# A causal linear attention with two expert layers behind it: earlier routing of the first token group, state products by halves

## The chip, the cores and the metric

The kernel runs on one core of one Trainium2 chip. The metric is the device time of one launch in microseconds (us); less is better. A time is the median of several runs, and a profile is one execution of its own.

## What is computed

The input of the expert layers is a gated linear attention: 4 batches of 8 heads, 768 positions, head size 48. Its output, 3072 rows of 384, goes through a layer of 8 experts of which each row takes the best two, and then through a gated product layer.

```python
for t in range(S):
    state = alpha[:, :, t, :, None] * state + np.einsum('bhd,bhe->bhde', k[:, :, t], v[:, :, t])
    y[:, :, t] = np.einsum('bhd,bhde->bhe', q[:, :, t], state)
...
logits = x @ w_gate
noise_scale = np.log1p(np.exp(x @ w_noise))
noisy_logits = logits + noise_scale * noise
top2 = np.argpartition(-noisy_logits, 2, axis=1)[:, :2]
...
    h = np.maximum(x[mask] @ w1[e], 0.0)
    out[mask] += top2_w[mask, k, None] * (h @ w2[e])
...
return (a * b @ w_out).astype(np.float32)      # a = x @ w_a, b = x @ w_b
```

## The kernel before

The order of all work is written out by hand: each engine runs its instructions in the order in which the program emits them, and waits only where data needs it.

**Attention.** The rows are cut into 24 tiles of 128 positions, six per batch. The loop over the tiles i emits for each: the load of tile i+5; `t_unit(i+1)`, four TensorE transposes of the keys (L664), with a filling product of no use (`fill`, L628) in front from tile `FILL` on; `gx_unit(i-1)`, three transposes of the output of the last tile (L749), likewise with a filling product; `inter(i)`, the queries times the state of the past (L688, the state lies as a block-diagonal copy `Sbd`, and it is left out for the first tile of a batch); `sc_unit(i+1)`, the scores (L672), masked by VectorE (L677); `prep(i+3)`, two scans on VectorE (L640, L644) and the products with them on GpSimd (L642, L645, L648); `intra(i)`, the masked scores times the values (L696); the copy of the output on ScalarE (L704); `gm_unit(i-1)`, the logits (L758), and their copy (`lg_unit`, L763, ScalarE); `sbd(i+1)`, two copies of the state into `Sbd` (L714, ScalarE); `u_unit(i+1)`, keys times values (L725); `s_unit(i+1)`, which adds them to the state on VectorE (L740, or L737 in a batch's first tile) and scales it on GpSimd (L741); and `w_tick(i)`, the split of an expert weight on ScalarE and GpSimd (L114, L115). A weight is split into a rounded part and a rest, as the expert products take three passes (L829 to L831).

**Routing beside it.** `routing(s)` is a Python generator. It joins a list when the logits of a subset of tiles are through: subset 0 is tiles 0 to 13, subset 1 tiles 14 to 18, subset 2 tiles 19 to 23. Each call of `tick` resumes every generator on the list up to its next `yield`, and so fixes where its instructions stand in the engines' queues. The loop calls `tick` four times a tile, numbered 0 to 3: ahead of `inter`, behind `prep`, ahead of `u_unit`, and behind `s_unit`. Write (i, k) for tick k of tile i. `choose` makes the noisy logits and the two best experts (ScalarE, then GpSimd, then VectorE; on VectorE alone for the last subset). `route` of a group (group 0 is subset 0, group 1 the other two) ranks its rows by a scan (L337) and products (L345 to L351), makes places from them (VectorE L356 to L384, TensorE L393), and gathers the rows of expert 0 with indirect DMAs that GpSimd issues (L493). `lists` makes the row lists of the other experts: equality tables on VectorE (L440, L444) and products (L460), whose sum goes into one accumulator (L463). `before_states` holds products back until tick 2 or the end of the loop. After the loop, `tick` is called from the expert units.

**Behind the loop.** `x_unit(0, j)` transposes a block of gathered rows (L501); blocks 0 and 1 stand inside tile 23, between `inter(23)` and `intra(23)`. Then come three filling products, the logits of tile 23, and expert 0 with its first 384 rows, `up_unit(0, f, 0)`, in which L829 starts.

```python
    def before_states():
        while phase[0] in (0, 1, 3):
            yield
...
    def tick(k=None):
        phase[0] = k
        for d in side[:]:
            if next(d, 0) == 0:
                side.remove(d)
```

Of the kernel before, what the change touches and what calls it, by code (L numbers as in the profile page):

```python
# [21 lines left out]
NT = B * NCH  # L22
# [20 lines left out]
LAG = 3  # L43
# [5 lines left out]
FILL = 13  # L49
# [12 lines left out]
def moe_kernel(ctx: ExitStack, tc, qka, afirst, v, wgn, noise, w1, w2, w3, out):  # L62
# [183 lines left out]
    def choose(s):  # L246
# [29 lines left out]
        for _ in hop(1):  # L276
            yield
        nc.scalar.activation(c, w, AF.Copy, bias=-1.0)
        nc.scalar.activation(mz, z, AF.Relu)
        for _ in hop(2, 1):  # L280
            yield
# [6 lines left out]
        for _ in hop(4):  # L288
            yield
# [3 lines left out]
        for k in range(2):  # L293
            eq = scr("eq", E)
            m, mk = (tl(rt, [128, MCH], F32, f"r_{x}{k}", bufs=2)[:, :n] for x in ("m", "mk"))
            o = oh[k][:, i0:i1]
            nc.vector.tensor_reduce(m, nl, axis=AX.X, op=ALU.max)
            for _ in hop(1):
                yield
            nc.vector.tensor_tensor(eq, nl, m[:, :, None].to_broadcast(sh), op=ALU.is_equal)  # L300
            nc.vector.tensor_tensor(eq, eq, prio[:, None, :].to_broadcast(sh), op=ALU.mult)
            for _ in hop(1):
                yield
            nc.vector.tensor_reduce(mk, eq, axis=AX.X, op=ALU.max)
            nc.vector.tensor_tensor(o, eq, mk[:, :, None].to_broadcast(sh), op=ALU.is_equal)
            yield
            if k == 0:
                nl2 = scr("nl2", E)
                nc.vector.scalar_tensor_tensor(nl2, o, -1e30, nl, op0=ALU.mult, op1=ALU.add)
                nl = nl2  # L310
            ms.append(m)
# [3 lines left out]
        for _ in hop(2, 1):  # L315
            yield

    def route(g):
# [21 lines left out]
        for _ in range(LAG + 1 if last else LAG):  # L340
            yield
# [46 lines left out]
        for _ in range(LAG - 1 if last else LAG):  # L388
            yield
# [31 lines left out]
    def lists(g):  # L421
# [27 lines left out]
        for s, after in zip(sets, sets[1:] + [None]):  # L449
# [6 lines left out]
            yield from before_states()  # L456
# [107 lines left out]
    def routing(s):  # L564
        yield from choose(s)
        g = group_of[CHS[s]][0]
        if CHS[s + 1] == groups[g][-1] + 1:
            yield from route(g)
            yield from lists(g)
# [14 lines left out]
    with ExitStack() as actx:  # L584
# [98 lines left out]
        def inter(i):  # L683

            PY[i] = bank(4)
            if i % NCH:
                for p in range(NP):
                    nc.tensor.matmul(PY[i][:, p * 96:p * 96 + 96], ring[i % RING][:, p * 128:p * 128 + 128],  # L688
                                     Sbd[i % 2][:, p], start=p == 0, stop=False, skip_group_check=True)
# [92 lines left out]
        for i in range(NT):  # L782
# [18 lines left out]
            x_out_unit(i)  # L801
            if i > 0:
                lg_unit(i - 1, gm_unit(i - 1))
            sbd(i + 1)
# [532 lines left out]
```

## Time and profile before

| | us |
|---|---|
| median of 3 runs (lowest, highest) | 1017.1 (1016.07, 1017.14) |
| the profiled execution | 1016.42 |
| its span, first to last instruction | 1014.6 |
| TensorE busy | 987.8 (97%) |
| VectorE busy | 557.0 (55%) |
| GpSimd busy | 416.4 (41%) |
| ScalarE busy | 376.1 (37%) |

The profile is of one execution. PE is TensorE's products, PEld its weight loads, DVE VectorE, ACT ScalarE, POOL GpSimd; L12 is line 12 of the program. A product of 32-bit floats has two records. Products overlap, so the time of one is better read from the start of one group to the start of the next. Attention ends, and expert 0 starts, at 138 us of the span.

### The profile page before, as it was taken

To read this page: it belongs to the slowest core of one execution; us is meant where nothing else is said; L and a number is where in the kernel's file an instruction comes from. 1 tells how busy PE (TensorE), PEld (TensorE's weight loads), DVE (VectorE), ACT (ScalarE), POOL (GpSimd) and SP (SyncE) were. 2 spreads that over 40 slices of the span, in tenths; PEclk is the share of its full clock that TensorE was granted. 3 is DMA by queue.
4 is the path that set the end of the run, shared out by engine and by line. 5 is a ranking of instruction groups with operands and counts; after the bars stand their busy time and mean duration, and the time that the engine had idled before them with its cause. 6 is when DMAs were issued, how large, how long until landed. Compare 5 with 4: busy or idle time off the path is not lost.

```text
span 1014.6 us, 17331 instructions
## 1 busy us (share of the span) xinstructions
PE 987.8 (97%) x6544; PEld 895.6 (88%) x6544; DVE 557.0 (55%) x967; ACT 376.1 (37%) x811; POOL 416.4 (41%) x433
## 2 busy tenths in 40 slices
PE   6999979999999999999999999999999999999997
PEld 5998868999999999999999888888888888888886
DVE  8998855576766776766756454333332333433221
ACT  2455521554545454545444343222222222222222
POOL 7688712575867685868564334020020110000000
PEclk9999989999999999999999999999999999999999
DMA  9787111668687868787856444140140240120100
GB/s 337 265 310 278 54 40 36 199 195 243 218 229 225 227 209 241 232 233 237 221 151 195 120 141 109 45 111 0 47 109 1 56 102 1 32 62 1 32 1 34
DMA packets 126549, 141.44 MB, mean 139 GB/s; under 512 B 76512, under 2 KB 110432, under 8 KB 126432
## 3 DMA queue, kind: packets, MB, share of 16 engines
q1 hardware_dynamic: 119904, 120.13, 39.6%
q0 software_dynamic: 6528, 19.67, 6.5%
q8 instruction: 83, 1.36, 0.6%
q14 instruction: 34, 0.28, 0.1%
HBM read 101.43 MB, written 38.34 MB: 138 GB/s over the span
## 4 chain that ended last, share of the span: by engine, by line
PE 83%; DVE 2%; DMA 1%; ACT 1%; issue 1%; POOL 0%; SPq 0%; DVEq 0%; ACTq 0%; POOLq 0%
PE bank L829 27%; PE bank L831 27%; PE bank L830 26%; DMA row<-xd,idx 1%; PE bank L501 1%; DMA wd<-w 1%; PE bank L696 1%; PE bank L460 0%; DVE HB L881 0%; PE bank L672 0%; PE bank L688 0%; PE bank L628 0%; DVE u L980 0%; ACT HB L880 0%; ACT o L1171 0%
## 5 line engine op out<-in xcount | busy, mean ns | idle before, releaser
L829 PE MATMUL bank<-HB,W 128*128 128x416 f32 (+5 forms) x564 | 201.3, 357 | 2.2 <-ACT HB L880 1.5
L831 PE MATMUL bank<-HB,W 128*128 128x416 f32 (+5 forms) x564 | 200.0, 355 | 0.0
L830 PE MATMUL bank<-HB,W 128*128 128x416 f32 (+5 forms) x564 | 199.8, 354 | 0.0
L115 POOL TENSOR_TENSOR W<-wst,W 128x384 fp32r<-128x384 f32 x136 | 146.8, 1088 | 91.9 <-ACT W L114 80.2
L1148 DVE TENSOR_TENSOR p<-bank,a 128x512 f32<-128x512 f32 x72 | 49.8, 692 | 236.1 <-PE bank L831 236.1
L829 PE MATMUL bank<-X,W 128*128 128x416 f32 (+6 forms) x474 | 166.3, 351 | 0.6 <-ACT X L503 0.4
L831 PE MATMUL bank<-X,W 128*128 128x416 f32 (+5 forms) x474 | 165.3, 349 | 0.0
L830 PE MATMUL bank<-X,W 128*128 128x416 f32 (+5 forms) x474 | 165.3, 349 | 0.0
L1010 POOL DMA_INDIRECT row<-y,row x48 | 46.3, 964 | 200.4 <-DVE row L1018 167.0
L829 PEld LDWEIGHTS bank<-HB,W 128*128 128x128 f32 x564 | 106.1, 188 | 9.8 <-ACT HB L880 2.6
L831 PEld LDWEIGHTS bank<-HB,W 128*128 128x128 f32 x564 | 105.9, 188 | 7.4 <-POOL W L115 0.2
L830 PEld LDWEIGHTS bank<-HB,W 128*128 128x128 f32 x564 | 106.0, 188 | 7.2
L1146 ACT ACTIVATE a<-bank 128x512 f32<-128x512 f32 x72 | 43.1, 598 | 168.5 <-PE bank L831 168.5
L1150 ACT ACTIVATE HB<-p 128x512 fp32r<-128x512 f32 x72 | 45.5, 632 | 157.6 <-DVE p L1148 157.6
L880 ACT ACTIVATE HB<-bank 128x416 fp32r<-128x416 f32 (+2 forms) x128 | 65.8, 517 | 100.7 <-PE bank L831 100.5
L829 PEld LDWEIGHTS bank<-X,W 128*128 128x128 f32 x474 | 89.1, 188 | 5.1 <-DVE HB L881 0.7
L881 DVE SCALAR_TENSOR_TENSOR HB<-bank,HB 128x416 fp32r<-128x416 f32 (+2 forms) x128 | 72.6, 582 | 36.9 <-ACT HB L880 36.3
L831 PEld LDWEIGHTS bank<-X,W 128*128 128x128 f32 x474 | 89.0, 188 | 3.9
L830 PEld LDWEIGHTS bank<-X,W 128*128 128x128 f32 x474 | 89.0, 188 | 3.8
L114 ACT ACTIVATE W<-wst 128x384 fp32r<-128x384 f32 x144 | 72.3, 516 | 17.4 <-DMA wst<-w 15.8
L493 POOL DMA_INDIRECT row<-xd,idx x56 | 57.8, 1033 | 47.9 <-DVE r_t L407 24.5
L1151 DVE TENSOR_TENSOR HB<-p,HB 128x512 fp32r<-128x512 f32 x72 | 49.8, 692 | 50.3 <-ACT HB L1150 50.3
(236 smaller groups left out, 1727.1 us busy)
## 6 DMA issues: line engine op xcount, KB each, us to landing
wst<-w SPq DMA_DIRECT2D x128, 192.0 KB, 4.5
ring<-qka SPq DMA_DIRECT2D x22, 768.0 KB, 6.3
wd<-w SPq DMA_DIRECT2D x36, 384.0 KB, 4.7
y<-o SPq DMA_DIRECT2D x56, 156.0 KB, 3.2
xt<-tb SPq DMA_DIRECT2D x11, 768.0 KB, 4.8
raw<-xt SPq DMA_DIRECT2D x44, 192.0 KB, 4.4
w3f<-u SPq DMA_DIRECT2D x36, 192.0 KB, 3.0
wst<-w3f SPq DMA_DIRECT2D x36, 192.0 KB, 3.2
```

The source lines that it names most:

```text
L114: nc.scalar.activation(h, raw, AF.Copy)
L115: eng.tensor_tensor(l, raw, h.bitcast(F32), op=ALU.subtract)
L493: nc.gpsimd.indirect_dma_start(out=t[:m], out_offset=None, in_=xd[:SPLIT * 128] if a else xd, in_offset=bass.IndirectOffsetOnAxis(ap=ix, a ...
L829: nc.tensor.matmul(ps[:, :m], ah, bh[:, :m], start=first, stop=False)
L830: nc.tensor.matmul(ps[:, :n], ah, bl[:, :n], start=False, stop=False)
L831: nc.tensor.matmul(ps[:, :n], al, bh[:, :n], start=False, stop=last)
L880: nc.scalar.activation(Hh[:, f, s], pu[:, :n], AF.Relu)
L881: nc.vector.scalar_tensor_tensor(Hl[:, f, s], pu[:, :n], 0.0, Hh[:, f, s].bitcast(F32), op0=ALU.max, op1=ALU.subtract)
L1010: nc.gpsimd.indirect_dma_start(out=t, out_offset=None, in_=src, in_offset=bass.IndirectOffsetOnAxis(ap=row[:, i, k:k + 1], axis=0))
L1148: nc.vector.tensor_tensor(p, ps[1], a, op=ALU.mult)
L1150: nc.scalar.activation(h, p, AF.Copy)
L1151: nc.vector.tensor_tensor(l, p, h.bitcast(F32), op=ALU.subtract)
```

## The change

`choose` yields less often for the subsets that aren't the last; `route` waits one tick less in two places of group 0; `lists` of group 0 waits for the end of the loop, and each set of a list but the last gives way for two ticks ahead of its product, in place of `before_states`. The filling products start at tile 17 instead of 13. `inter` does each product as two of 64 queries. The copy of the logits is emitted behind the copies into `Sbd`.

```diff
-FILL = 13
+FILL = 17
@@ choose
         nc.scalar.activation(r, ln, AF.Exp, scale=-1.0)
-        for _ in hop(1):
-            yield
         nc.scalar.activation(c, w, AF.Copy, bias=-1.0)
         nc.scalar.activation(mz, z, AF.Relu)
-        for _ in hop(2, 1):
+        for _ in hop(1, 1):
             yield
...
-        for _ in hop(4):
+        for _ in hop(3):
             yield
...
             nc.vector.tensor_reduce(m, nl, axis=AX.X, op=ALU.max)
-            for _ in hop(1):
-                yield
             nc.vector.tensor_tensor(eq, nl, m[:, :, None].to_broadcast(sh), op=ALU.is_equal)
             nc.vector.tensor_tensor(eq, eq, prio[:, None, :].to_broadcast(sh), op=ALU.mult)
-            for _ in hop(1):
-                yield
             nc.vector.tensor_reduce(mk, eq, axis=AX.X, op=ALU.max)
             nc.vector.tensor_tensor(o, eq, mk[:, :, None].to_broadcast(sh), op=ALU.is_equal)
-            yield
+            if k == 0 or last:
+                yield
...
-        for _ in hop(2, 1):
+        for _ in hop(1, 1):
             yield
@@ route
-        for _ in range(LAG + 1 if last else LAG):
+        for _ in range(LAG + 1 if last else LAG - 1):
             yield
...
-        for _ in range(LAG - 1 if last else LAG):
+        for _ in range(LAG - 1):
             yield
@@ lists
             m, at, bt = hot.pop(s)
-            yield from before_states()
+            if s[1] != NT:
+                yield
+                yield
@@ routing
             yield from route(g)
+            while phase[0] is not None:
+                yield
             yield from lists(g)
@@ inter
-                    nc.tensor.matmul(PY[i][:, p * 96:p * 96 + 96], ring[i % RING][:, p * 128:p * 128 + 128],
-                                     Sbd[i % 2][:, p], start=p == 0, stop=False, skip_group_check=True)
+                    for t in (0, 64):
+                        nc.tensor.matmul(PY[i][t:t + 64, p * 96:p * 96 + 96],
+                                         ring[i % RING][:, p * 128 + t:p * 128 + t + 64],
+                                         Sbd[i % 2][:, p], start=p == 0, stop=False, skip_group_check=True)
@@ the loop over the tiles
-            if i > 0:
-                lg_unit(i - 1, gm_unit(i - 1))
-            sbd(i + 1)
+            pg = gm_unit(i - 1) if i > 0 else None
+            sbd(i + 1)
+            if i > 0:
+                lg_unit(i - 1, pg)
```

## Rows read from the trace of the kernel before

**Rows 1.** TensorE's waits: who it waited for; us in total, times, longest.

```profile
PE bank L501 <- DMA row<-xd,idx: 3.1, 2, 2.4
PE bank L688 <- ACT Sbd L714: 2.0, 3, 1.0
...
PE bank L460 <- DVE lacc L463: 1.1, 1, 1.1
```

**Rows 2.** Timeline of TensorE, 107 to 165 us: start, us, what [idle before <-releaser].

```profile
121.76 1.03 PE L688 MATMUL bank<-Sbd,ring 128*128 128x96 f32 x8
...
125.20 0.91 PE L393 MATMUL bank<-bt,at 128*128 128x7 f16 x14
...
131.23 0.89 PE L501 MATMUL bank<-ident,row 128*128 128x128 f32 x3 [0.66 <-DMA row<-xd,idx]
...
138.16 0.44 PE L829 MATMUL bank<-X,W 128*128 128x384 f32 x1
...
143.80 1.09 PE L460 MATMUL bank<-bt,at 128*128 128x49 f16 x10 [1.19 <-DVE bt L444]
...
158.73 0.41 PE L829 MATMUL bank<-HB,W 128*128 128x384 f32 x1 [0.70 <-DVE idx L397]
```

**Rows 3.** Windows of 1 us: busy us by engine, then granted clock, DMA, GB/s.

```profile
109.00:110.00 1.00, 0.34 (x4) 0.10 (x1) 1.00 (x3) 0.70 (x2) 1.00 (x2) 1.00 0.67 209
...
131.00:132.00 1.00, 0.77 (x3) 0.52 (x3) 0.56 (x1) 0.10 (x1) 0.00 (x0) 0.50 0.54 169
...
137.00:138.00 1.00, 1.00 (x12) 0.30 (x12) 1.00 (x5) 0.08 (x1) 0.00 (x0) 0.63 0.00 0
```

**Rows 4.** Timeline of GpSimd, 85 to 180 us.

```profile
94.49 1.27 POOL L642 TENSOR_TENSOR ring<-ring,D 128x512 f32<-128x512 f32 x1
...
115.99 1.28 POOL L642 TENSOR_TENSOR ring<-ring,D 128x512 f32<-128x512 f32 x1
...
118.80 0.51 POOL L741 TENSOR_TENSOR sc<-ss,aend 128x192 f32<-128x192 f32 x1
119.27 0.27 POOL L282 TENSOR_TENSOR r_c<-r_c,r_ex 128x40 f32<-128x40 f32 x1
...
126.60 1.13 POOL L493 DMA_INDIRECT row<-xd,idx  x1 [2.37 <-DVE bank L309]
...
130.26 0.43 POOL L407 TENSOR_TENSOR r_t<-oh,r_rs 128x112 f32<-128x112 f32 x1
```

**Rows 5.** Timeline of VectorE, 78 to 124 us.

```profile
90.46 1.29 DVE L677 TENSOR_TENSOR pm<-bank,causal 128x512 f32<-128x512 f32 x2 [0.71 <-PE bank L672]
...
94.56 1.33 DVE L291 TENSOR_TENSOR bank<-r_sp,LG 128x112 f32<-128x112 f32 x1
...
108.66 0.41 DVE L337 TENSOR_TENSOR_SCAN xc<-bank,oa 128x120 f32<-128x120 f32 x1 [1.25 <-POOL oa L313]
...
117.44 0.17 DVE L356 CAST bank<-bank 128x14 int32<-128x14 f32 x1
...
119.85 1.27 DVE L677 TENSOR_TENSOR pm<-bank,causal 128x512 f32<-128x512 f32 x2
121.04 1.38 DVE L384 TENSOR_TENSOR at<-lane,r_pf 128x896 f16<-128x896 f16 x2
```

**Rows 6.** Timeline of TensorE in tile 14, 78 to 83 us.

```profile
78.23 1.03 PE L688 MATMUL bank<-Sbd,ring 128*128 128x96 f32 x8
79.19 1.16 PE L672 MATMUL bank<-ring 48*128 48x128 f32 x16
80.28 1.14 PE L696 MATMUL bank<-v,pm 128*64 128x48 f32 x32
81.25 0.49 PE L758 MATMUL bank<-wgn,gx 128*64 128x16 f32 x12
...
82.06 0.39 PE L628 MATMUL bank<-junk 128*128 128x512 bf16 x1
82.28 0.60 PE L664 MATMUL bank<-ident,ring 128*128 128x128 f32 x4
```

## The prediction

> **What bounds the kernel now.** The list of what TensorE waited for comes first. After the 3.4 us before its first instruction, its longest entry is 3.1 us in two waits of L501 for the gathered rows [rows 1]. The timeline of TensorE places it: the state product of tile 22 starts at 121.76, the list product L393 at 125.20, the second transpose of gathered rows only at 131.23, and expert 0 at 138.16 [rows 2]. The windows of 1 us show a second loss there: the granted clock is 0.95 of full speed at 130 to 131, 0.50 (the 1.2 GHz level) from 131 on, in six such rows, and 0.63 at 137 to 138 [rows 3]. That is some 6.7 us at half speed, so 3.3 us lost. GpSimd shows why the rows are late: it issues the three gathers from 126.60 on and is through at 130.26, 3.66 us [rows 4]. The rest of attention goes at the pace of several engines. VectorE's queue has from 90.46 to 117.44 only one wait that the timeline names, the 1.25 us ahead of L337 [rows 5], so there VectorE sets the pace. Expert 0 has two more waits, 1.2 and 1.1 us, for the lists' tables and their sum [rows 1, 2].
>
> **The steps, counted.** The routing of group 0 joins the ticks at tile 14, tick 2. Its n-th piece runs at tick (n+1) mod 4 of tile 14 + floor((n+1)/4). Before, the count gives the rank products at (20,2), L393 at (22,2) and the gathers at (23,0), as the timelines have it. After, nine yields ahead of the first scan L337 are gone, so that it is piece 10 instead of 19, and two of the waiting yields behind it; the rank products come at (17,2), L393 at (19,2), the gathers at (20,0). The lists of group 0, before spread from tick 2 after the loop, begin at the first tick after the loop, and each set's product two ticks after its table.
>
> **Early gathers, gain.** The rows land long before tile 23. That removes the 3.1 us, and L393 leaves the last stretch (0.8 us from its start to what follows). If nothing else came late, the fall of the clock would go too, 3.3 us.
>
> **Early gathers, price on VectorE.** Between 90.46 and 117.44 it now also does the rank and key pieces, 2.4 us (117.44 to 119.85), and the two place tables, 1.4 us; of the 1.25 us wait before the scan some 0.8 us may go, because L313 is issued in the piece before [rows 5]. That is 3.0 us more in a queue that sets the pace. Against it stands what TensorE gains before tile 16 (next two parts), at most 2.9 us, of which I take 2.5. The queue can use it: it waited 0.71 us for TensorE in a tile [rows 5]. So VectorE reaches the end of tile 19 about 0.5 us later than before.
>
> **Early gathers, price on GpSimd.** This is the term that I weigh most. At (20,0) the three gathers stand in GpSimd's queue in front of the products of prep(23) and the state's product L741 of tile 20. Before, prep(23) started at 115.99 and L741 at 118.80 [rows 4]. Now 3.66 us of gathers come first, and then, ahead of L741 too, L407 (0.43) and five small products of the second subset (L282 to L287, 0.27 each with 0.06 between, 1.6 us), whose ticks are now (20,1) and (20,2). With the 0.5 us of VectorE that is 6.2 us: L741 starts at 125.0 and ends at 125.5. The two copies into the block-diagonal state take 0.7 us behind it, so the state product of tile 22 starts at 126.2 where it started at 121.76. TensorE's transposes of tile 23 wait before that for prep(23). Thus a wait of some 5 us in two pieces replaces that of 3.1 us.
>
> **The last stretch.** From 121.76 to 138.16 are 16.4 us [rows 2]. Less 3.1, 3.3, 0.8 and 0.2 (halves of two tiles) that is 9.0 us at full clock: expert 0 would start at 135.2. The old wait of 3.1 us was enough for the clock to fall; the new one is longer, so I let it fall. How much of the half-speed time lies beside the wait the trace doesn't show: between half of before's loss, 1.7 us, and all of it, 3.3. I take 2.5, since the fall may come while TensorE still waits. Expert 0 then starts at 137.7, 0.5 us earlier than before.
>
> **Filling products.** At tiles 13 to 16 eight products L628 are left out. One takes 0.22 us from its start to the next line [rows 6]; seven lie before VectorE's saturated stretch: 1.5 us. Nothing hides them where TensorE sets the pace. What they cover is the clock: without them TensorE has more idle time at tile 17, where five softplus products of GpSimd (some 0.43 us each, as L407 has it for that size), now ahead of L741 at tile 15, hold up the state by some 2 us [rows 4]. Waits of L688 of up to 1.0 us, as at 109 to 110, left the clock at full speed [rows 1, 3], so I price this at nothing for the clock and let VectorE's queue hide the wait itself.
>
> **State products by halves.** Eight records of full width take 0.96 us to the next line, 0.11 each with the change of shape behind them; L696, half as wide, takes 0.97 us for 16 pairs, 0.06 a pair [rows 6]. A new pair lies between 0.06 (the width of what is loaded sets it) and 0.11 (L672 takes that for a pair of full width). By 96 against its 128 columns it is 0.083: 8 x 0.083 is 0.66 against 0.88 us. The change from the full-width transposes in front to half width costs between 0.08 (0.96 less 8 x 0.11) and 0.21 us (1.09 less 0.88, behind L672). I take 0.1 us saved per tile, ends +0.4 and -0.2; on 14 tiles before tile 17 at most 1.4 us. The Trainium skill (TensorEngine Tiling, Key Properties) says that a change of tiling mode drains TensorE; the rows agree with that extra time, and by the dearer end the halves would save nothing and the sum would be 1.4 us worse.
>
> **Logits behind the copies.** L763 (0.18 us) moves behind two copies on ScalarE. Where the state comes late, the logits, the W split and two PSUM copies behind them wait; TensorE waits for the same state, so nothing is added. Its gain is below 0.1 us a tile.
>
> **Lists.** Their tables start two ticks earlier relative to their products, and products get two ticks more. The waits of 1.2 and 1.1 us go [rows 1, 2]; late next is the rank product of the last group, behind the same VectorE queue: up to 0.75 us. I take 2.0 us saved of the 20.6 us from 138.16 to 158.73 [rows 2], ends 1.0 and 2.5. Expert 1's gathers come two ticks, about 1 us, later; they have time.
>
> **Sum.** 0.5 + 2.0 = 2.5 us. Behind 158.73 TensorE is dense and all of it stays. The profiled execution had 1016.4 us (span 1014.6, 1.8 around it); the median, 1017.1, is 0.7 above it. So 1013.9 against its own, and 1014.6 for the median.
>
> **Rivals.** (a) *The new wait doesn't slow the clock.* For it: nothing shows that a wait always does. Against it: 3.1 us sufficed. Expert 0 at 135.2 and 2.0 us of lists: 5.0 us gained, 1012.1. (b) *VectorE gets further ahead.* If its queue is 3 us earlier at tile 19, GpSimd is too, and the clock holds: expert 0 at 132.2, 8.0 us gained, 1009.1. Against it: the queue has 3 us more to do. (c) *The halves don't pay.* If a pair takes 0.11 and each change of shape 0.21, tile 16 comes 1.4 us later than I have it: 1016.0, no difference to be seen. (d) *Slower: VectorE and GpSimd shut each other out.* L291, which reads two SBUF operands, took 1.33 us where its like take 0.27, exactly while L642 ran (94.49 to 95.76) [rows 4, 5]: 1.06 us lost. Eight such instructions of the first group now fall into tiles 16 to 18, where GpSimd works most of the time; my sum has two of them waiting, as before. Each more costs up to 1.06 us in the queue that sets the pace, so from three on the change is slower than before; all six give 1014.6 + 6.4 = 1021.0. Against it: at 117.44 to 122.4 the same kinds waited little. The Trainium skill (SBUF — State Buffer, Who interferes with whom) says that such an instruction and a reading GpSimd one exclude each other for their whole length; by that rule any of the eight can wait.
>
> **Numbers.** The forecast has a chance of 0.50, own range 1012.5 to 1017.5; (a) 0.20, (b) 0.10, (c) 0.08, (d) 0.12. A difference of 0.2%, 2.0 us, is about what measurement can tell from none; the line is at 1015.1. Of the forecast's 0.50, 0.28 lie below it, 0.20 within and 0.02 above. So faster 0.58, same 0.28, slower 0.14. The range takes in (a), most of (b) and the near part of (d): 1008.5 to 1020.
>
> **What would show it.** Right: gathers on GpSimd some 10 us earlier than 126.60 and no wait of L501 for them; a wait of L688 for the copies L714 of 3 us or more at tile 22, behind L741 behind the gathers; half speed after it; sixteen L688 records a tile in under 0.9 us; the two waits of L460 gone. Wrong: L688 of tile 22 near 122 (then (a) or (b)), a clock that stays full, VectorE instructions with two SBUF operands of over 0.5 us in numbers (d), or half speed already at tile 17.

## The result, and the profile of the changed kernel

| | before | changed |
|---|---|---|
| median of 6 runs each, us | 1015.91 | 1028.07 |
| lowest, highest | 1014.95, 1017.14 | 1022.29, 1030.33 |
| the profiled execution | 1016.42 | 1022.29 |
| its span | 1014.6 | 1020.5 |

The ratio is 1.0119, with a 95% interval of 1.0101 to 1.0137: the change makes the kernel 12 us slower. The profiled execution is the fastest of the six of the changed kernel, and also the one with the highest mean granted clock, 0.991; the others had 0.984 to 0.990. What a profile of it shows is therefore the smaller part of the loss: 5.9 of the 12.2 us.

The list of what TensorE waited for, in the first 170 us of the changed kernel (us in total, times, longest). L750 writes the transposes of the output, L627 is the filling product in front of it, L388 is the list product that was L393, L764 is the logits' copy.

```profile
PE bank L750 <- ACT LG L764: 5.3, 9, 2.3
...
PE bank L627 <- ACT LG L764: 2.8, 2, 2.1
PE bank L388 <- DVE ss L741: 1.3, 1, 1.3
PE bank L388 <- DVE lacc L460: 1.3, 1, 1.3
```

The waits of [rows 1] for the rows (3.1), for `Sbd` (2.0) and of L460 for `lacc` (1.1) are not in it; but L388 of the second group now waits 1.3 us for `lacc`. In their place stand 8.1 us in eleven waits for the logits' copy, which the list of before does not have.

TensorE's timeline shows where (start, us, what, and in brackets the wait ahead of it). These lines answer to [rows 2] and [rows 6].

```profile
76.69 0.88 PE L688 MATMUL bank<-Sbd,ring 128*64 128x96 f32 x16
77.50 1.16 PE L671 MATMUL bank<-ring 48*128 48x128 f32 x16
...
81.48 0.55 PE L750 MATMUL bank<-ident,x 128*128 128x128 f32 x3 [0.45 <-ACT LG L764]
81.95 0.88 PE L688 MATMUL bank<-Sbd,ring 128*64 128x96 f32 x16
...
98.22 0.55 PE L750 MATMUL bank<-ident,x 128*128 128x128 f32 x3 [2.26 <-ACT LG L764]
...
102.71 0.39 PE L340 MATMUL bank<-xc,ones 128*128 128x8 f32 x2 [0.64 <-DVE xc L332]
...
116.33 0.87 PE L388 MATMUL bank<-bt,at 128*128 128x7 f16 x14 [1.31 <-DVE ss L741]
...
133.29 0.38 PE L627 MATMUL bank<-junk 128*128 128x512 bf16 x1 [2.10 <-ACT LG L764]
...
146.25 0.44 PE L831 MATMUL bank<-X,W 128*128 128x384 f32 x1
...
165.80 0.66 PE L831 MATMUL bank<-HB,W 128*128 128x384 f32 x1 [0.59 <-DVE r_t L402]
```

Tiles 13 and 14, in the quiet middle, stand at the top: they are 5.26 us apart (76.69 to 81.95), and 0.45 of it is the wait of L750. Then come the large waits: 2.26 us at tile 17, 1.31 at tile 19, 2.10 at tile 22. Expert 0 starts at 146.25 (138.16 before), the second product of the expert at 165.80 (158.73).

Windows of TensorE's clock (the columns of [rows 3]: the seventh value is the granted clock), 1 us each for the first lines, then 10 us:

```profile
103.00:104.00 1.00, 1.00 (x7) 0.81 (x7) 0.96 (x4) 0.00 (x0) 0.34 (x1) 0.97 0.94 326
104.00:105.00 1.00, 1.00 (x18) 0.82 (x18) 1.00 (x1) 0.00 (x0) 0.00 (x0) 0.50 0.91 250
...
130.00:140.00 10.00, 7.90 (x106) 6.82 (x103) 6.29 (x20) 3.76 (x11) 5.13 (x13) 0.73 0.11 42
...
160.00:170.00 10.00, 8.13 (x48) 7.72 (x48) 5.17 (x19) 0.98 (x2) 3.40 (x4) 0.83 0.15 42
```

The clock is at its lower level (0.50, 1.2 GHz) three times before expert 0: from 103.9, from 117.6 and from 134.7, some 13.7 us in all, so 6.8 us lost; and once more from 165.4. Before, it was one stretch of 6.8 us, 3.4 lost [rows 3]. So of the 8.1 us by which expert 0 comes later, 3.4 are clock. The other 4.7 are the new waits, less what is saved: the wait for the rows, the halves and the filling products left out.

ScalarE's timeline between those two tiles shows the logits' copy L764 behind the copies of the state, and these behind GpSimd:

```profile
79.78 0.49 ACT L705 ACTIVATE x<-bank 128x384 f32<-128x384 f32 x1 [2.21 <-PE bank L697]
80.48 0.73 ACT L715 ACTIVATE Sbd<-sc 64x192 f32<-64x192 f32 x2 [0.21 <-POOL sc L742]
81.24 0.18 ACT L764 ACTIVATE LG<-bank 128x16 f32<-128x16 f32 x1
```

The copy ends at 81.42 and L750 starts at 81.48. Right behind L705 it would have ended some 0.9 us earlier (0.21 and 0.73).

GpSimd's timeline, to [rows 4]:

```profile
94.30 0.42 POOL L280 TENSOR_TENSOR r_c<-r_c,r_ex 128x112 f32<-128x112 f32 x1
...
96.68 0.51 POOL L742 TENSOR_TENSOR sc<-ss,aend 128x192 f32<-128x192 f32 x1
...
123.49 1.13 POOL L490 DMA_INDIRECT row<-xd,idx  x1 [0.17 <-issue]
...
127.15 1.28 POOL L641 TENSOR_TENSOR ring<-ring,D 128x512 f32<-128x512 f32 x1
...
129.77 0.41 POOL L402 TENSOR_TENSOR r_t<-oh,r_rs 128x112 f32<-128x112 f32 x1
130.15 0.26 POOL L280 TENSOR_TENSOR r_c<-r_c,r_ex 128x40 f32<-128x40 f32 x1
...
131.76 0.51 POOL L742 TENSOR_TENSOR sc<-ss,aend 128x192 f32<-128x192 f32 x1
```

The five softplus products of the first subset stand ahead of the state's product (96.68), and the two copies and the logits' copy behind that end as L750 starts, at 98.22. At tile 20 the three gathers stand first, then prep(23), L402, five small products and the state's product at 131.76: the order that the prediction had counted.

### The profile page after: what moved, and what is told of

It reads as the page before. It is cut to its first block, busy times and chain, and to the rows that moved or that the text cites. A ratio compares the mean times of both kernels' runs of the same rounds, so it can differ in the third digit from the quotient of the medians.

```text
span 1020.5 us, 17632 instructions
## 1 busy us (share of the span) xinstructions
PE 996.4 (98%) x6696; PEld 897.7 (88%) x6696; DVE 558.8 (55%) x967; ACT 377.4 (37%) x811; POOL 416.4 (41%) x433
## 3 DMA queue, kind: packets, MB, share of 16 engines
q8 instruction: 84, 1.38, 0.6%
## 4 chain that ended last, share of the span: by engine, by line
PE 84%; DVE 2%; issue 1%; ACT 1%; POOL 1%; another core or an unknown queue 0%; DVEq 0%; POOLq 0%
PE bank L831 27%; PE bank L832 27%; PE bank L833 27%; PE bank L498 1%; PE bank L457 0%; PE bank L688 0%; PE bank L671 0%; PE bank L697 0%; POOL row L490 0%; ACT o L1173 0%; DVE HB L883 0%; PE bank L627 0%; DVE W L115 0%; DVE row L1020 0%
## 5 line engine op out<-in xcount | busy, mean ns | idle before, releaser
L831 PE MATMUL bank<-HB,W 128*128 128x416 f32 (+5 forms) x564 | 202.0, 358 | 0.6 <-DVE r_t L402 0.6
L831 PE MATMUL bank<-X,W 128*128 128x416 f32 (+6 forms) x474 | 166.3, 351 | 0.4 <-ACT X L500 0.4
L831 PEld LDWEIGHTS bank<-HB,W 128*128 128x128 f32 x564 | 106.5, 189 | 8.4 <-issue 1.0
L831 PEld LDWEIGHTS bank<-X,W 128*128 128x128 f32 x474 | 89.1, 188 | 4.6 <-ACT X L500 0.6
```

What stands on the lines that cost most here:

```text
L831: nc.tensor.matmul(ps[:, :m], ah, bh[:, :m], start=first, stop=False)
```

## The experiments

Each was timed beside runs of the kernel before on the same chip. Where no ratio is named, a gain or loss in us is the difference of the two medians there; runs on different chips are compared by their ratios, of which 0.001 is 1 us. The table gives, for some, the start of the masked products (L696 of before) of a tile minus that of before, read from TensorE's timelines, and where the clock fell between tile 2 and expert 0. Tile 2 shows what an execution is off from its start on.

| kernel | ratio | tile 2 | 11 | 16 | 18 | 20 | 22 | expert 0 | half speed from |
|---|---|---|---|---|---|---|---|---|---|
| before | 1 | 24.8 | 66.5 | 90.4 | 99.2 | 112.2 | 123.8 | 138.2 | 130.9 |
| changed | 1.0119 | +0.9 | +3.4 | +3.4 | +9.3 | +10.2 | +12.9 | +8.1 | 103.9, 117.6, 134.7 |
| e1 logits alone | 1.0066 | +0.2 | +3.1 | +3.7 | +4.2 | +4.3 | +4.4 | +4.5 | 135.8 |
| e2 all but logits | 1.0028 | -0.1 | -1.3 | -2.5 | +5.0 | +3.2 | +7.4 | +3.2 | 93.3, 127.4 |
| e3 halves alone | 0.9986 | -0.1 | -1.3 | -1.5 | -1.5 | -1.6 | -1.8 | -1.8 | 129.0 |
| e4 routing alone | 1.0039 | -0.3 | -0.3 | -0.3 | +4.1 | +7.4 | +7.7 | +1.6 | 112.0 |
| e13 e4, tables later | 0.9997 | 0.0 | 0.0 | 0.0 | +4.3 | +3.0 | +3.9 | -1.1 | none |
| e14 spare tables | 1.0041 | +0.6 | +0.6 | +0.6 | +0.6 | +3.4 | +3.4 | +3.5 | 110.8, 134.7 |
| e11 two ticks | 0.9955 | +0.9 | -0.2 | -0.5 | +0.2 | +0.4 | +3.6 | -2.5 | 122.1 |

### One part at a time

**The logits' copy alone (e1)**, on the kernel before:

```diff
-            if i > 0:
-                lg_unit(i - 1, gm_unit(i - 1))
+            pg = gm_unit(i - 1) if i > 0 else None
             sbd(i + 1)
+            if i > 0:
+                lg_unit(i - 1, pg)
```

> The kernel before with one edit: the copy of the logits behind the two copies into the block-diagonal state. Theory P (the logits lie in the PSUM bank that the next tile's transposes L750 write; so these wait until the logits are copied, and that copy now stands behind 0.7 us of copies and behind whatever those wait for): a tile without filling products takes 5.0 us instead of 4.65, L750 waits for the logits' copy in most tiles, intra of tile 11 starts 3 to 4 us later than at 66.46; some of it is hidden where VectorE sets the pace; 1019 to 1024 us. Rival Q (ScalarE has room, the order of the copies costs nothing, as the prediction had it): no wait of L750, tile 11 within 0.5 us of 66.46, 1016 us.

Measured: 1019.99 us, ratio 1.0066 (1.0042 to 1.0091), 6.0 us lost (6.7 by the ratio): theory P. TensorE's waits:

```profile
PE bank L749 <- ACT LG L763: 3.2, 7, 0.9
...
PE bank L628 <- ACT LG L763: 1.8, 2, 1.5
```

Nothing but the place of one 0.18 us copy differs. `trbank` hands out two PSUM banks in turn, and a tile takes both: one for the transposes of its keys, one for those of the output and, in free columns, the logits. So the next tile's transposes L749 write the bank in which the logits lie, and the waits show that they start only when the copy has read it. TensorE waits for the copy, not for the state.

**The changed kernel with the copy put back (e2)**, the reverse of that edit:

> The changed kernel with only the copy of the logits put back ahead of the copies into the block-diagonal state. Theory P: the waits of L750 go, a tile takes 4.5 to 4.6 us at tiles 2 to 11, and what is left is the prediction's sum: 1010 to 1018 us. Rival Q: the loss of 12 us comes from the routing and from the filling products alone, and stays: 1024 to 1028 us.

Measured: 1018.14 us, 1.0028 (1.0007 to 1.0049): theory P, at the upper edge of its range. Putting the one copy back gains 9.1 thousandths of the changed kernel's 11.9. Tile 16 is 2.5 us earlier than before, which is what the prediction's sum took for it; by tile 18 that is gone. At tile 17 the state's product starts behind a wait of 1.91 us, as GpSimd's five softplus products stand ahead of the state, and the clock is at half speed from 93.3 to beyond 103 (TensorE's timeline, then windows of 1 us):

```profile
92.32 0.88 PE L688 MATMUL bank<-Sbd,ring 128*64 128x96 f32 x16 [1.91 <-ACT Sbd L715]
```

```profile
94.00:95.00 1.00, 1.00 (x12) 0.81 (x8) 0.90 (x4) 0.00 (x0) 1.00 (x2) 0.50 0.03 12
```

At tile 22 stands the wait that the prediction weighed most. GpSimd issues the three gathers from 118.12 on; prep(23), L402 and five small products follow, and the state's product starts only at 126.36. TensorE waits for the copies behind it, and the clock is at half speed from 127.4 on (GpSimd, then TensorE):

```profile
126.36 0.51 POOL L742 TENSOR_TENSOR sc<-ss,aend 128x192 f32<-128x192 f32 x1
...
127.69 1.55 PE L688 MATMUL bank<-Sbd,ring 128*64 128x96 f32 x16 [3.38 <-ACT Sbd L715]
```

**The halves alone (e3)**, the hunk of `inter`:

> The kernel before with one edit: the state products by halves of 64 queries. In the changed kernel sixteen records take 0.81 us to the next line instead of 0.96 for eight, and the first of them starts 0.48 us behind the first of the three transposes where it was 0.33. Theory H1 (the halves give 0.15 us a tile and lose as much at the change of shape ahead of them): 0 to 1 us, 1015 to 1017. Theory H2 (the prediction's 0.1 us a tile is kept): intra of tile 11 some 1.0 us earlier than at 66.46, 1014 to 1015. Rival H3 (the halves themselves lengthen a tile): 1017 to 1019.

Measured: 1012.89 us, 0.9986 (0.9972 to 1.0000), 1.1 us gained; in the profile 1.4 us by tile 16, 0.1 a tile, as in theory H2.

**The routing alone (e4)**: the changed kernel with three parts undone.

```diff
-FILL = 17
+FILL = 13
-                    for t in (0, 64):
...
+            if i > 0:
+                lg_unit(i - 1, gm_unit(i - 1))
             sbd(i + 1)
```

> The kernel before with the routing edits alone (fewer steps for group 0, its lists after the loop); products of full width, filling products from tile 13, logits' copy in its old place. Theory G (GpSimd's queue: the three gathers and five small products ahead of the state's product of tile 20): the gathers start near 118, L688 of tile 22 waits some 3 us or more for the state, the clock falls again, expert 0 starts between 136 and 141 us, lists gain 1 to 2.5 us: 1014 to 1019 us. Rival V (VectorE's 3 us more in a queue that sets the pace is hidden): expert 0 before 133 us, 1009 to 1011 us. Rival W (the change of the clock in tiles 17 to 22 is the main loss): half speed shows ahead of tile 20, 1019 us or more.

Measured: 1017.31 us, 1.0039 (1.0024 to 1.0053), 3.4 us lost, though the waits for the rows are gone. No theory held as it stood: the wait at tile 22 is 1.50 us and not 3 (G), and half speed comes ahead of tile 20, as in W, at less than W's 1019 us. The timeline of VectorE (L736 and L739 are the sums for the state, L379 the place tables) and of TensorE:

```profile
102.80 0.33 DVE L736 TENSOR_TENSOR sc<-bank,aend 128x192 f32<-128x192 f32 x1
...
109.93 2.34 DVE L379 TENSOR_TENSOR at<-lane,r_pf 128x896 f16<-128x896 f16 x2
112.19 0.34 DVE L739 TENSOR_TENSOR ss<-bank,sc 128x192 f32<-128x192 f32 x1
...
112.59 0.86 PE L388 MATMUL bank<-bt,at 128*128 128x7 f16 x14 [2.77 <-DVE ss L739]
```

The view of the tables' tile (ns: shortest, median, longest; the median is a wider table of the second group):

```profile
L379 DVE TENSOR_TENSOR at<-lane,r_pf x3: 668/819/1754, 109.9 to 154.3; 128x896 f16<-128x896 f16 x2, 128x1280 f16<-128x1280 f16 x1
```

The sum for tile 19 comes 9.4 us behind that for tile 18 (102.80 to 112.19). In the kernel before the same two stand here (VectorE, then TensorE behind the second):

```profile
101.22 0.35 DVE L737 TENSOR_TENSOR sc<-bank,aend 128x192 f32<-128x192 f32 x1
...
107.07 0.35 DVE L740 TENSOR_TENSOR ss<-bank,sc 128x192 f32<-128x192 f32 x1
...
107.47 0.56 PE L725 MATMUL bank<-v,kn 128*48 128x48 f32 x16 [0.63 <-DVE ss L740]
```

5.9 us, and TensorE already waited 0.63 for it: there was no slack at that place. The list product waits for the sum as the transposes wait for the logits, since it writes the bank that the sum reads.

**The filling products alone (e5)**: `FILL = 17` in the kernel before.

> The kernel before with one edit: filling products from tile 17 instead of 13. Theory F1 (the fall of the clock needs a long wait behind it, and the kernel before has none of over 1.2 us ahead of tile 21): full clock up to tile 21, intra of tile 16 some 1.3 us earlier than in the kernel before, part of it lost again to VectorE: 0 to 1.5 us faster. Rival F2 (the filling products themselves hold the clock in tiles 13 to 20): half speed shows between tiles 14 and 20, 1 to 4 us slower.

Measured: 1014.48 us, 0.9991 (0.9980 to 1.0002), 1.0 us gained, not told from none; between tiles 11 and 16 its timeline goes from 0.5 us behind the kernel before to 0.3 ahead, and no fall of the clock is added behind tile 2.

### What makes the logits' copy dear

**Columns of another bank for the logits (e6)**, in the changed kernel:

```diff
-pg = PX.pop(i)[:, DM:DM + 2 * E]
+pg = UG[:, 480:480 + 2 * E]
```

> The changed kernel, logits' copy still behind the copies into the block-diagonal state, but the logits written into columns of their own in bank 6 (480 to 495) instead of the bank that the next transposes need. Theory P (the bank is what makes L750 wait): no wait of L750 for the logits' copy, tiles 2 to 11 at 4.5 to 4.65 us, total as with the copy put back, 1016 to 1020 us. Rival Q2 (the late copy itself, or ScalarE's order, costs the time by another way): tiles 2 to 11 still at 4.95 us or more, 1023 us or more.

Measured: 1038.07 us, 1.0224 (1.0198 to 1.0249), far worse than expected. The wait of L750 is gone and another has come (TensorE's waits, then a line of its timeline):

```profile
PE bank L726 <- ACT LG L764: 19.4, 16, 3.9
...
67.81 0.56 PE L726 MATMUL bank<-v,kn 128*48 128x48 f32 x16 [1.10 <-ACT LG L764]
```

The columns were free, but the bank was not: `u_unit` writes it right behind the logits' product. So in both kernels the product that next writes the bank waits for the late copy; here that product comes sooner, and the waits are longer. The Trainium skill (PSUM — Partial Sum Buffer, PSUM bank collisions raise a hardware error) says that access to PSUM is to be guarded by bank and quadrant (32 partitions), or simply by bank, and not by address. The trace shows this program waiting so: 1.10 us at 67.81 for columns that no one else touched.

### What makes the routing dear

**Gathers held back (e7)**, in the routing alone (e4); `now` is the tile:

```diff
+        while not last and phase[0] is not None and (now[0] < 21 or phase[0] != 3):
+            yield
         for j in range(*mine.indices(NJ)):
             gather(0, j)
```

> The routing edits alone as in the run with them alone, but the three gathers of group 0 held until tick 3 of tile 21, behind the last state product that they held up. Theory G (GpSimd's queue): L741 of tile 20 comes 3.7 us earlier, the wait of L688 at tile 22 shrinks below 0.5 us, no fall of the clock behind it, expert 0 starts 1.5 to 4 us earlier than with the routing edits alone: 1012.5 to 1016 us. Rival V2 (VectorE's queue alone sets tiles 20 to 22): within 0.5 us of the routing edits alone, 1016.5 to 1018.

Measured: 1021.55 us, 1.0060 (1.0043 to 1.0076), no gain. Tile 20 is 8.2 us late before any gather is issued (they come from 132.1 on). The wait at tile 22 does shrink, from 1.50 to 0.47 us, but at tile 23 one of 1.98 us takes the place of 0.65. So in e4, where the time up to tile 20 is lost before, the gathers' place ahead of the state's product is not what costs the 3.4 us.

**Softplus products two ticks later (e8)**, in e4:

```diff
-        for _ in hop(1, 1):
+        for _ in hop(3, 1):
             yield
         eng.tensor_tensor(c, c, ex, op=ALU.subtract)
...
-        for _ in hop(3):
+        for _ in hop(1):
             yield
```

> The routing edits alone, but the five softplus products of GpSimd two ticks later, behind the state's product of their tile (two ticks fewer behind them, so that all else stands as with the routing edits alone). Theory G2 (they hold up the state at tile 17 and at tile 22): the waits of L688 at tiles 17 (1.4 us) and 22 go or fall below 0.7 us; VectorE, whose products wait for them at (16,1), takes the time back: 0 to 1.5 us faster than the routing edits alone, 1016 to 1017.5. Rival: the wait at tile 17 stays, as the state is late for another reason.

Measured: 1023.11 us, 1.0074 (1.0051 to 1.0096), slower and not faster than e4. The wait for the state at tile 17 is gone, but the rank products now wait for VectorE, 3.9 us in one piece (L340 for the scan L332), and the clock falls twice. Two waits of e4, 1.43 us at tile 17 for GpSimd and 1.07 us for the scan behind it, have become one: GpSimd's wait had stood in front of VectorE's. Some 1.0 us is new, as L289 on VectorE takes 1.34 us beside GpSimd's L641 and had taken 0.34.

**Place tables four ticks later (e13)**, in e4:

```diff
         yield
+        if not last:
+            for _ in range(4):
+                yield
         for j0 in range(0, n, m):
             at = hot_tile("at", 128, m)
```

> The routing's edits alone, with one edit against them: group 0's place tables on VectorE stand four ticks later, so at ticks 1 and 2 of tile 19 in place of tile 18, the list product one tile later, at (20,2), and the gathers at (21,0). With the routing's edits alone the sum for the state of tile 19 came on VectorE at 112.19 in place of 107.07, the list product waited 2.8 us for it, and the clock fell at 112.0 for 6.8 us. Theory V (the tables, 2.3 us in front of the state's sum in a queue that is already late, cause that wait and that fall): the sum comes near 110, the wait there is gone or below 1 us, no half speed before 115, tile 20 at +3 or less in place of +7.4, and a ratio of 1.000 to 1.002. Rival (VectorE is late by the choice's twelve pieces and the ranks' keys, with or without the tables): the sum above 111, a wait of 2 us or more at tile 18 or 19 all the same, ratio 1.003 to 1.005.

Measured: 1017.16 us, 0.9997 (0.9982 to 1.0013): the routing's loss is gone. The sum for tile 19 comes at 110.17 and TensorE waits 0.50 us for it:

```profile
110.17 0.33 DVE L742 TENSOR_TENSOR ss<-bank,sc 128x192 f32<-128x192 f32 x1
...
110.56 0.56 PE L727 MATMUL bank<-v,kn 128*48 128x48 f32 x16 [0.50 <-DVE ss L742]
```

The granted clock is 1.00 in every window from 106 to 138. Theory V held, with a ratio just below its range. The tables now stand in front of the next tile's sum (116.74) with their 2.35 us, and TensorE waits 0.40 us there. Tile 18 is still 4.3 us late, behind the choice's pieces and the softplus products, and expert 0 starts 1.1 us earlier than before all the same. This run moves the list product and the gathers too; that the tables by themselves cost such a loss is what the next one shows.

**Spare tables in the kernel before (e14)**; the same three lines stand once more behind tick 2.

```diff
             tick(1)
+            if i == 18:
+                sp_ = hot_tile("at", 128, 7)
+                nc.vector.tensor_tensor(sp_, lane[:, :, :7], keys[:, None, 0, :7].to_broadcast([128, 128, 7]),
+                                        op=ALU.is_equal)
             intra(i)
```

> The kernel before with two throwaway equality tables (128x896, f16) on VectorE at ticks 1 and 2 of tile 18, where the changed kernel makes its place tables; nothing reads them, and they add work that the reference doesn't need. This measures by itself what some 1.4 to 2.3 us more on VectorE cost at this place. Theory V (VectorE sets the pace there): the state's sums behind them come 1.4 to 2.3 us later than 107.07 and 112.96, TensorE waits longer by as much, in one piece, at tiles 19 and 20; ratio 1.001 to 1.002, and 1.004 to 1.006 if the clock falls for it. Rival (VectorE has room: it waited 1.25 us ahead of the first scan): no later than tile 20, ratio 0.999 to 1.001.

Measured: 1019.78 us, 1.0041 (1.0020 to 1.0063). The timeline of VectorE, of GpSimd beside it, and of TensorE:

```profile
107.71 1.56 DVE L802 TENSOR_TENSOR at<-lane,keys 128x896 f16<-128x896 f16 x1
109.19 0.68 DVE L812 TENSOR_TENSOR at<-lane,keys 128x896 f16<-128x896 f16 x1
109.79 0.35 DVE L740 TENSOR_TENSOR ss<-bank,sc 128x192 f32<-128x192 f32 x1
...
107.46 1.26 POOL L645 TENSOR_TENSOR ring<-ring,A 128x512 f32<-128x512 f32 x1 [0.22 <-DVE A L644]
108.68 0.65 POOL L648 TENSOR_TENSOR aend<-af,D 128x4 f32<-128x4 f32 x1
...
110.19 0.56 PE L725 MATMUL bank<-v,kn 128*48 128x48 f32 x16 [2.72 <-DVE ss L740]
```

2.1 us of VectorE (109.79 less 107.71) make a wait of 2.72 us where 0.63 stood, and the clock falls at 110.8. Two tables that nothing reads cost 4.2 us by the ratio (3.2 by the medians), as much as the whole routing (4.0 by its ratio). Theory V held.

### The filling products and the clock

**e9**, the changed kernel with `FILL = 13`:

> The changed kernel with one part undone: the filling products start at tile 13 again. Alone, on the kernel before, their removal had gained 1.0 us. Theory C (their worth is the clock: once TensorE waits in tiles 17 to 22, eight products more keep it from falling as often): fewer or shorter stretches at half speed than the 3.4, 3.4 and 6.8 us of the changed kernel up to expert 0, and a time of 1022 to 1026. Rival (the price of a filling product is only its own 0.22 us): the same stretches, tile 16 later by some 0.7 us, since the filling product in front of the output's transposes lies beside their wait, and a time about 1 us above the changed kernel's, 1027 to 1029.

Measured: 1024.39 us, 1.0097 (1.0067 to 1.0127). The stretch from 103.9 is missing, two remain ahead of expert 0 (theory C); tile 16 is 0.7 us later, as the rival had it, 0.3 of it from tile 2 on. By itself the difference of 2.2 us is not settled, as the intervals overlap.

**e10**, the changed kernel with `FILL = 13` and the logits' copy put back:

> The changed kernel with two parts undone: the filling products start at tile 13 and the logits' copy stands ahead of the copies of the state. What is left is the routing in fewer steps and the products by halves. Alone the first cost 3.4 us and the second gained 1.1, so if they don't touch each other: ratio 1.002, some 1017. Theory C (without filling products the clock falls earlier and longer): about 2 us faster than the same kernel with the filling products from 17 on, which stood at 1.0028, and no half speed before 105 us. Rival (the early tiles get ahead by the halves and then wait longer for the state at tiles 17 to 20, whatever the filling products do): 1.003 or more, with the offset of tile 16 of -1.5 us gone by tile 18.

Measured: 1016.01 us, 1.0013 (1.0000 to 1.0025), 1.5 us better than e2 by the ratios, with overlapping intervals; but the clock falls at 101.0 all the same, so theory C did not hold as it stood. At tile 22 TensorE waits 3.38 us, as in e2.

**e12**, the kernel before with the logits' copy moved and `FILL = 17`:

> The kernel before with two parts of the change: the logits' copy behind the copies of the state, and the filling products from tile 17 on. Alone the first cost 6.0 us and the second gained 1.0. If they don't touch each other: ratio 1.005, tile 16 some 3 us later, no half speed before 120 us. If the filling products are what keeps the clock up once TensorE waits in each tile (theory C): half speed between 90 and 125 us, and a ratio of 1.008 or more.

Measured: 1019.78 us, 1.0051 (1.0031 to 1.0071): the sum of the two parts, although its profiled execution, with 1023.30 us the second slowest of ten, was at half speed from 113.6 on.

**e11**, the kernel before with the halves, and the noisy logits two ticks earlier:

```diff
-        for _ in hop(4):
+        for _ in hop(2):
             yield
```

> The kernel before with two edits: its products with the state by halves, and the four ticks between GpSimd's softplus products and the noisy logits cut to two, so that the ranks of group 0 come at (19,2), L393 at (21,2) and the gathers at (22,0); nothing else of the routing moves. If the gain of early gathers is real and only the neighbourhood of the changed kernel's place costs it (the tick (20,0) stands ahead of GpSimd's product for the state of tile 22, the tick (22,0) behind it), the waits of 3.1 us for the rows and the half speed at 131 to 138 go and nothing takes their place: expert 0 at 131 to 134 in place of 138.16, and a ratio of 0.993 to 0.996. If VectorE's queue at tiles 17 to 20 is the cause of the routing's loss, each piece that moves into it costs the same here: expert 0 at 136 to 139, ratio 0.998 to 1.002.

Measured: 1010.63 us, 0.9955 (0.9941 to 0.9970), 4.4 us faster than the kernel before and, by the ratios, some 17 faster than the changed one. Expert 0 starts at 135.64, between the two expectations; the ratio is in the range of the first. The gathers come at 126.9, behind GpSimd's last product for a state that is read. That is no earlier than before (126.60): the rows are there for L501 because it starts only at 130.61. The tables, at a later tile, cost a wait of 2.28 us and one fall of the clock, at 122.1. So the gain is not shown to be that of earlier gathers. Up to expert 0, and less what the two executions differ by at tile 2, it is 3.4 us; the halves alone gave 1.7 (e3), and the clock loses 1.7 us here for 3.4 before.

**e15**, e11 with `FILL = 17`:

> The version with two ticks fewer and the products by halves (ratio 0.9955), with the filling products from tile 17 on. Alone on the kernel before, this gained 1.0 us; beside the whole routing it cost 1.5 to 2.2 us. If what decides is whether TensorE has a wait of over 2 us at tiles 17 to 20, which this version does not have: 0.994 to 0.996, about 1 us better. If the clock falls as soon as these products are gone and any routing comes earlier: half speed between 90 and 110 us and 0.997 to 0.999.

Measured: 1014.71 us, 0.9981 (0.9964 to 0.9999), 2.6 us worse than e11 by the ratios. At tile 17 both wait 1.62 us for the same sum. First e11, a line of TensorE's timeline and two windows of 1 us, then the same of e15:

```profile
102.50 0.56 PE L727 MATMUL bank<-v,kn 128*48 128x48 f32 x16 [1.62 <-DVE sc L739]
```

```profile
102.00:103.00 1.00, 0.50 (x17) 0.45 (x17) 0.97 (x5) 0.44 (x2) 1.00 (x3) 1.00 0.00 0
103.00:104.00 1.00, 1.00 (x12) 0.84 (x9) 1.00 (x2) 0.89 (x3) 1.00 (x3) 1.00 0.00 0
```

```profile
100.55 0.88 PE L727 MATMUL bank<-v,kn 128*48 128x48 f32 x16 [1.62 <-DVE sc L739]
```

```profile
100.00:101.00 1.00, 0.45 (x12) 0.45 (x14) 0.97 (x5) 0.39 (x2) 1.00 (x3) 0.59 0.00 0
101.00:102.00 1.00, 1.00 (x15) 0.71 (x12) 1.00 (x2) 0.86 (x2) 1.00 (x3) 0.50 0.00 0
```

Behind the same wait the clock stays at 1.00 with the filling products of tiles 13 to 16 and falls to 0.50 without them. It is one execution of each, and e15 had another 0.61 us of wait 4 us earlier (0.17 in e11). Nor is this fall all of e15's loss in its profile: at tile 23 TensorE waits 2.30 us for ScalarE's L706, which waited for something that the profile doesn't show, and e11 has no such wait. Over the pairs, whose intervals overlap each time, the sign agrees by the ratios: where the routing comes earlier, leaving the filling products out costs 1.5 (e2 against e10), 2.2 (changed against e9) and 2.6 us (e15 against e11); where it doesn't, it gains 0.9 (e5) and 1.5 (e12 against e1).

## Why the prediction was wrong, step by step

**Logits behind the copies** is the step that failed first and most. It said "TensorE waits for the same state, so nothing is added". It looked for who waits for the copy's result and not for who waits for the bank that the copy reads: the transposes of the next tile, which stand in front of the state's product. It was priced at nothing and measured 6.0 us alone (e1) and 9.1 thousandths, 9.2 us, in the changed kernel (against e2). None of the rivals had it either; the slower one was another mechanism.

**Early gathers, price on VectorE** had the right work and the wrong sum. It spread 3.0 us over the tiles up to 19, set 2.5 us of gain against them, and had the queue 0.5 us late. In e4 the choice's twelve pieces, before spread from 94.56 to 107.15, stand in one block from 94.19 to 97.96, with the scan and the masks behind them; tile 18 is 4.1 us late, after waits of 1.43 us (GpSimd) and 1.07 us (the scan). Then the place tables fall into one tile, in front of the state's sum, where TensorE already waited 0.63 us; the sum for tile 19 comes 5.1 us later than before (112.19 for 107.07), the wait is 2.77 us, and the clock falls at it. In e13, without the tables there, the sum is still 3.1 us late, so some 2.0 us are the tables'. e13 and e14 show this cause from both sides for the routing alone. Two terms were also too small: the tables took 2.34 us where [rows 5] have 1.38 for L384, and the rank and key pieces 2.9 us (103.30 to 106.18 in e13) where the step had 2.4. This part of rival (d) was right: the first table took 1.75 us and the second 0.67 in e4, where GpSimd ran L644 beside the first. The Trainium skill (SBUF — State Buffer, Who interferes with whom) says that a VectorE instruction with two inputs in SBUF contends with a GpSimd instruction that reads SBUF. The rows agree, and show both delayed: the first table took some 1.1 us longer than the second, and L644 beside it 1.56 us for 1.27.

**Early gathers, gain** held in its parts: no wait of L501 for the rows in the changed kernel, and none in e11. But the gathers come 3.1 us earlier (123.49 for 126.60) and not some 10, as all ahead of them is late. **Price on GpSimd** was right in mechanism: gathers, prep(23), L402, five small products, the state's product, and the wait behind it at tile 22. With the logits' copy put back the size is near too: in e2 the wait is 3.38 us, with 0.49 for prep(23) ahead of it, for some 5 in two pieces, TensorE goes on at 127.69 for 126.2, and half speed follows. What the step didn't see is the loss ahead of it, and the wait is the shorter the later TensorE comes to it: in e2 it is there at 124.31 and goes on at 127.69; in e4, after 2.77 us at the tables' sum and half speed, it is there at 127.83 and goes on at 129.33, and e7 shows that later gathers gain nothing. In the changed kernel the wait at tile 22 is 2.10 us, through the logits' copy.

**The last stretch** and **Filling products** took one fall of the clock, at the place of the old one, and priced the filling products at nothing for it. That fall came (134.7), but there were three, the first at 103.9 behind 2.26 and 0.64 us of waits. The row that it leaned on was misread: the wait at 109 to 110 is 0.74 us, and the one of 1.02 us stands at tile 2 (22.64). The sentence on tile 17 (softplus products ahead of the state hold it up by some 2 us) was right: 1.91 us in e2. Letting VectorE's queue hide that wait and leaving the clock at full speed was not: half speed at tile 17, which the prediction named as a sign of being wrong, is there in e2 (93.3). The products' own price of 1.5 us measured 1.0 (e5); beside the earlier routing leaving them out cost 1.5 to 2.6 us in each of three pairs, none of them settled alone. That this is the clock is what e9 and e15 point to, and not shown.

**State products by halves** was right: sixteen records take 0.81 us to the next line where eight took 0.96 [rows 6], and the part gained 1.1 us for the 1.4 at most that the step allowed. What follows the change of shape costs a part of it back: in the changed kernel L688 starts 0.47 us behind L750 (81.48 to 81.95), and in the kernel before 0.33 us behind the same transposes (121.43 to 121.76). **The sum of these steps** up to tile 16, 2.5 us, came out in e2 (2.5, or 2.4 from tile 2 on).

**Lists** were put at 2.0 us; from expert 0 to the second product are 19.55 us in the changed kernel for 20.57, so 1.0. The new order isn't needed for it: e11 has the old order and 19.38. And the changed kernel has new waits there, 1.29 us of L388 for `lacc` and 0.59 of L831, with half speed from 165.4 on, about 1.7 us lost; e4 and e13 fall there too (159.8, 156.7), and so do e1 and e14 with the old order (149.4, 148.3); e11 doesn't. Of the 7.1 us by which the second product comes later, 5.9 are left at the end of this execution.

**The account.** Three of the runs make a chain from before to changed, in which each kernel has one part more than the last. In thousandths of the time the halves give -1.4 (e3), the routing on top of them +2.7 (e10 against e3), the filling products +1.5 (e2 against e10) and the logits' copy +9.1 (changed against e2): +11.9, or 12.1 us. In other company the parts have other sizes. The logits' copy costs 6.6 alone (e1), 6.0 beside the filling products left out (e12 against e5) and 8.4 beside routing and halves (e9 against e10); the routing costs 3.9 alone (e4), and the filling products give -0.9 alone (e5). So the copy is the largest part each time. Whether the routing makes it dearer is not settled, as the intervals, 1 to 3 thousandths to either side, overlap.

## What to carry to other kernels

Before an instruction is moved back in its queue, ask not only who waits for what it writes but who is next to write what it reads: in these kernels a product into any column of a PSUM bank waited until the last reader of that bank was through (L749 in e1, L726 in e6). Where a row already shows a short wait for an engine (0.63 us here), that place has no slack: in e14 work put in front of it there cost its whole length, though the same queue had waited 1.25 us a little later. A piece of work that moves earlier is best put where little waits behind it: in e13 the tables stand a tile later, and TensorE waits only 0.40 us for the sum behind them. A wait that is small in one run (1.50 us at tile 22 in e4) can be large once the loss ahead of it is gone (3.38 us in e2). Filling products are judged together with the waits that follow them.

## What the runs showed of the hardware that was not expected

- Free columns in a PSUM bank were no place for a late reader: TensorE's waits for the logits' copy grew from 8.1 us in the changed kernel to over 19.4 in e6.
- A wait of 1.62 us left the granted clock at 1.00 in e11 and was followed by 0.50 in e15. Filling products in the tiles before it or none was the difference made between the two programs; e15 also had 0.61 us of wait ahead of it. One execution of each is too few to call it shown.
- Of two equal f16 equality tables of 128x896 the one beside a GpSimd product of 128x512 took 1.56 to 1.76 us and the other 0.67. GpSimd's own 0.20 us instruction, which ran beside both, took 0.65 there.
- Six executions of the changed kernel spread over 8 us with mean granted clocks of 0.984 to 0.991. The kernel before spread over 2 us in its six and over 4 to 5 us in the 16 to 25 beside each set of experiments. So how often the clock falls differs from one execution to the next, and a profile shows one of them.
